# A gated state-space and MLP mix on one core: set-up transposes moved from TensorE to transposing DMAs, and PSUM tiles regrouped

## The chip, the cores and the metric

The kernel runs on one core of a Trainium2 chip. Times are device microseconds (us) of one execution, given as the median of several. Every experiment was run beside the kernel before on the same chip. A ratio is the mean time of one kernel's fast runs over the mean of the other's fast runs of the same rounds, so it is not quite the ratio of the medians quoted. Executions over 1.5% slower than the fastest of the same kernel are left out of the means.

Engine names: PE is TensorE, PEld its weight loads, ACT is ScalarE, DVE is VectorE, POOL is GpSimd, SP is SyncE, which here only issues DMAs. "ACTq" and "SPq" are the queues from which ACT and SP issue DMAs.

## The reference, cut to what matters

```python
def reference(x, ...):                    # x: 2048 rows x 640, bf16
    g = sigmoid((x * gate_w).sum(-1))     # one gate per row
    # a: complex linear recurrence with 640 states
    h[t] = Lam_bar * h[t-1] + B_bar @ x[t]
    a = 2 * real(C @ h) + x * Dskip
    # b: MLP 640 -> 1728 -> 640 with tanh-GELU
    b = gelu(x @ w1 + b1) @ w2 + b2
    return g * a + (1 - g) * b
```

## The kernel before

Set-up ("the head") loads all inputs, brings x, B and C into transposed form, and makes tables of sines and cosines that turn the complex recurrence into two real scans. Then four groups of 512 rows follow ("the main part"). Each group does the MLP's first product in 14 chunks (`ph`), its activation (`xb`, `x2`, `u`, `sg`, `h1T`), the second product (`pb`, `bg`), five state-space blocks (`ps_bu`, `BB`, `M`, `V`, the scans `GG`, `hTg`), and the last product with the combine (`pa`, `o_sb`). The program is written in that order; a scheduler in the programming framework then places the instructions of each engine in a fixed order.

```python
# loads: ACT's queue issues four, SP's queue four
for hf in range(2):
    (nc.sync if hf == 0 else nc.scalar).dma_start(x_sb[:], x_v[:, hf*HT:(hf+1)*HT, :])
for part, src in enumerate((A_B_re, A_B_im)):
    (nc.sync if part == 0 else nc.scalar).dma_start(b_sb[:], ...)
nc.sync.dma_start(w1_sb...); nc.scalar.dma_start(w2_sb...)
for part, src in enumerate((A_C_re, A_C_im)):
    (nc.sync if part == 0 else nc.scalar).dma_start(c_sb[:], ...)
# ... tables: 10 rounds of ACT ang, four DVE steps, ACT Sin ...
# ... x: 80 PE transposes, PSUM copies by DVE (first half) and ACT (second half)
for part in range(2):                      # B: 50 PE transposes, 10 ACT copies
    for dc in range(NDC):
        for pc in range(NPC):
            nc.tensor.transpose(tp[:, pc*P:(pc+1)*P], b_sb[:, pc, dc*P:(dc+1)*P], ident_bf[:])
        nc.scalar.copy(BT[:, dc, part*NS:(part+1)*NS], tp[:, 0:NS])
# ... C: 50 PE transposes, 10 ACT copies into CT; then CpT from CT (ACT scale, DVE add) ...

# main part
pb = psum_b.tile([P, HALF], F32, name="pb")        # two one-bank buffers, one per half
...
nc.scalar.activation(bg[:, cols], pb[:], AF.Copy, scale=omg[:])
...
pa = psum_a.tile([P, HALF], F32, name="pa")        # one one-bank buffer
...                                                # 10 matmuls + 3 for the skip term
nc.vector.scalar_tensor_tensor(out=o_sb[:, cols], in0=pa[:], scalar=gcol[:], in1=bg[:, cols], ...)
```

Of the kernel before, what the change touches and what calls it, by code (L numbers as in the profile page):

```python
# [9 lines left out]
BF16 = mybir.dt.bfloat16  # L10
F32 = mybir.dt.float32
ALU = mybir.AluOpType
# [8 lines left out]
H1_MULT_ENGINE = "vector"  # L21
X2_ENGINE = "act"
COMBINE_MODE = "dve"
# [19 lines left out]
def kernel(  # L43
# [19 lines left out]
    nc = tc.nc  # L63
# [23 lines left out]

    pool_eng = nc.gpsimd
# [10 lines left out]
    ident_bf = const.tile([P, P], BF16, name="ident_bf")  # L99
    b1c = const.tile([P, NFC], F32, name="b1c")  # L100
# [9 lines left out]
    psum_t_cm = tc.tile_pool(name="psum_t", bufs=3, space=bass.MemoryType.PSUM)  # L110
# [26 lines left out]
    x_sbs = []  # L137
    for hf in range(2):
        x_sb = setup.tile([P, HT, D], BF16, name=f"x_sb{hf}")
        (nc.sync if hf == 0 else nc.scalar).dma_start(x_sb[:], x_v[:, hf * HT:(hf + 1) * HT, :])  # L140
        x_sbs.append(x_sb)
    b_sbs = []
    for part, src in enumerate((A_B_re, A_B_im)):
        b_sb = setup.tile([P, NPC, D], BF16, name=f"b_sb{part}")
        (nc.sync if part == 0 else nc.scalar).dma_start(b_sb[:], src.rearrange("(c p) d -> p c d", p=P))
        b_sbs.append(b_sb)
    nc.sync.dma_start(w1_sb[:, :, 0:F], B_w1.rearrange("(c p) f -> p c f", p=P))
    nc.scalar.dma_start(w2_sb[:, 0:NFULL, :], B_w2[0:NFULL * P, :].rearrange("(c p) d -> p c d", p=P))
    c_sbs = []
    for part, src in enumerate((A_C_re, A_C_im)):  # L150
        c_sb = setup.tile([P, NDC, NS], BF16, name=f"c_sb{part}")
        (nc.sync if part == 0 else nc.scalar).dma_start(c_sb[:], src.rearrange("(c p) s -> p c s", p=P))
        c_sbs.append(c_sb)
# [3 lines left out]
    nc.vector.tensor_copy(ident_bf[:], ident[:])  # L157

# [91 lines left out]
    for hf in range(2):  # L250
        x_sb = x_sbs[hf]
        for dc in range(NDC):
            tp = psum_t.tile([P, HT * P], BF16, name="tp")
            for i in range(HT):
                nc.tensor.transpose(tp[:, i * P:(i + 1) * P], x_sb[:, i, dc * P:(dc + 1) * P], ident_bf[:])  # L255
            if hf == 0:
                nc.vector.tensor_copy(xT[:, dc, hf * HT * P:(hf + 1) * HT * P], tp[:])
            else:
                nc.scalar.copy(xT[:, dc, hf * HT * P:(hf + 1) * HT * P], tp[:])

    for part in range(2):
        b_sb = b_sbs[part]
        for dc in range(NDC):
            tp = psum_t.tile([P, HT * P], BF16, name="tp")
            for pc in range(NPC):
                nc.tensor.transpose(tp[:, pc * P:(pc + 1) * P], b_sb[:, pc, dc * P:(dc + 1) * P], ident_bf[:])
            nc.scalar.copy(BT[:, dc, part * NS:(part + 1) * NS], tp[:, 0:NS])

# [7 lines left out]
    CT = setup.tile([P, NPC, 2 * D], BF16, name="CT")  # L276
    for part in range(2):
        c_sb = c_sbs[part]
        for pc in range(NPC):
            tp = psum_t.tile([P, HT * P], BF16, name="tp")  # L280
            for dcb in range(NDC):
                nc.tensor.transpose(tp[:, dcb * P:(dcb + 1) * P], c_sb[:, dcb, pc * P:(pc + 1) * P], ident_bf[:])
            nc.scalar.copy(CT[:, pc, part * D:(part + 1) * D], tp[:, 0:D])
    for pc in range(NPC):
        ctre = CT[:, pc, 0:D]
        ctim = CT[:, pc, D:2 * D]
        t1 = small.tile([P, D], F32, name="cpt_t1")
# [29 lines left out]

    def ssm_block(pc, tci, hTg):
        tcols = slice(tci * TCW, (tci + 1) * TCW)
        ps = []  # L320
        for part in range(2):
            pt = psum_bu.tile([P, TCW], F32, name=f"ps_bu{part}")
            for dc in range(NDC):
# [172 lines left out]
```

## Time and profile before

| | before |
|---|---|
| time, median of 6 runs | 330.69 us |
| ACT's first computing instruction (Exp) | 25.6 us |
| first `xb`, end of the head | 70.5 us |
| main part, from first `xb` to the end of the span | 258.8 us |

The page of the profiled run: busy time by engine, and the span cut into 40 slices of 8.2 us, with the busy share of each slice in tenths.

```profile
PE 247.3 (75%) x1583; PEld 146.2 (44%) x1604; DVE 240.0 (73%) x474; ACT 184.0 (56%) x341; POOL 14.7 (4%) x24
PE   0132554839999989999997989899889999940574
DVE  2508774485999997668979999982999858199322
ACT  0007999979995268687255685633577574320000
PEclk9999955789999999999999999999999999995599
DMA  7999100000000000100000000100000100000011
```

ACT does nothing for three slices and is then nearly full for the rest of the head; PE fills up from the ninth slice on and DVE from the eleventh.

The timeline (start, duration, engine, line, operation, output and input) says why ACT starts late:

```profile
1.99 5.21 ACTq L148 DMA_DIRECT2D w_sb<-in_B_w_dram  x1
7.23 17.04 ACTq L152 DMA_DIRECT2D c_sb<-in_A_C_im_dram  x1
24.30 1.28 ACT L160 ACT_TABLE_LOAD   x1 [24.30 <-issue]
70.51 0.69 ACT L388 ACTIVATE xb<-ph,b1c 128x512 bf16<-128x512 f32 x1 [1.80 <-issue]
```

The issue of the load of C holds ACT's own queue for 17 us, while the DMA engines work off what was issued before it. ACT computes nothing until that issue is through.

The view by windows (stretch, its length, busy us of PE, PEld, DVE, ACT and POOL, granted clock, DMA share, GB/s) for parts of the head and for the end:

```profile
40.00:50.00 10.00, 5.04 (x40) 4.22 (x40) 6.97 (x16) 9.97 (x17) 0.00 (x0) 0.52 0.00 0
50.00:60.00 10.00, 5.63 (x48) 4.95 (x48) 3.48 (x8) 9.96 (x18) 0.00 (x0) 0.50 0.00 1
290.00:310.00 20.00, 5.14 (x24) 2.35 (x23) 17.02 (x22) 1.13 (x2) 0.00 (x0) 0.66 0.00 0
```

From 40 to 60 us ACT is busy 19.9 of 20 us, so ACT sets the length of the head. Part of that work is copying transposes out of PSUM, as the groups by form show (count, total busy, mean ns):

```profile
L267 ACT COPY BT<-tp 128x640 bf16<-128x640 bf16 x10 | 6.3, 710 | 0.0
L283 ACT COPY CT<-tp 128x640 bf16<-128x640 bf16 x10 | 6.1, 722 | 0.0
L259 ACT COPY xT<-tp 128x1024 bf16<-128x1024 bf16 x5 | 4.9, 1005 | 1.2 <-PE tp L255 1.2
```

### The profile page before, as it was taken

Reading aid. Unit: us, or ns where it says so; the run is one execution under the profiler, and the core shown is the slowest. Engines: PE = TensorE matmul, PEld = TensorE weight load, DVE = VectorE, ACT = ScalarE, POOL = GpSimd, SP = SyncE. Lnnn points to the kernel's source line nnn. Section 1 sums busy time; section 2 is a strip of 40 time slices with the busy share of each in tenths; the row PEclk is TensorE's granted clock in tenths of the full one; section 3 lists DMA queues with packets and bytes.
Section 4 is the critical chain, followed back from the end, with each engine's and each line's share of the span. In section 5 each row is a group of like instructions: output and inputs, shape, how many; then the busy total and the mean of one; then the engine's idle time right before and its main releaser. Section 6 shows DMA issues by size and latency. Waiting matters only on the chain.

```text
span 329.3 us, 4218 instructions
## 1 busy us (share of the span) xinstructions
PE 247.3 (75%) x1583; PEld 146.2 (44%) x1604; DVE 240.0 (73%) x474; ACT 184.0 (56%) x341; POOL 14.7 (4%) x24
## 2 busy tenths in 40 slices
PE   0132554839999989999997989899889999940574
PEld 0132443514335735656743355566445556610353
DVE  2508774485999997668979999982999858199322
ACT  0007999979995268687255685633577574320000
POOL 8710000000000000000000000000000000000000
PEclk9999955789999999999999999999999999995599
DMA  7999100000000000100000000100000100000011
GB/s 218 223 396 365 57 0 1 0 0 2 0 0 3 0 2 21 41 21 0 2 0 1 2 20 20 42 0 3 0 0 22 41 22 0 0 2 0 0 40 40
DMA packets 9667, 13.21 MB, mean 40 GB/s; under 512 B 672, under 2 KB 8992, under 8 KB 9648
## 3 DMA queue, kind: packets, MB, share of 16 engines
q1 hardware_dynamic: 5312, 7.78, 6.9%
q10 hardware_dynamic: 4032, 5.08, 5.1%
q0 software_dynamic: 304, 0.09, 0.5%
q8 instruction: 12, 0.20, 0.2%
q14 instruction: 7, 0.06, 0.1%
HBM read 10.33 MB, written 2.62 MB: 39 GB/s over the span
## 4 chain that ended last, share of the span: by engine, by line
DVE 42%; PE 30%; ACT 4%; issue 2%; ACTq 0%
PE pb L420 12%; PE pa L434 8%; DVE GG L357 6%; DVE u L395 6%; DVE GG L359 6%; PE ph L380 5%; PE ps_bu L324 3%; DVE V L341 3%; DVE o_sb L454 3%; DVE h1T L400 3%; DVE M L338 3%; DVE M L339 3%; DVE N L367 3%; DVE hTg L369 3%; DVE N L368 3%
## 5 line engine op out<-in xcount | busy, mean ns | idle before, releaser
L380 PE MATMUL ph<-xT,w_sb 128*128 128x512 bf16 x269 | 68.5, 384 | 8.9 <-ACT x L391 7.0
L434 PE MATMUL pa<-CpT,hTg 128*128 128x320 bf16 x320 | 52.8, 309 | 24.2 <-DVE hTg L369 17.4
L420 PE MATMUL pb<-w_sb,h1T 128*128 128x320 bf16 x448 | 67.4, 299 | 4.9 <-DVE h1T L400 4.6
L420 PEld LDWEIGHTS <-h1T 128*128 128x128 bf16 x448 | 41.7, 98 | 32.2 <-DVE h1T L400 15.4
L434 PEld LDWEIGHTS <-hTg 128*128 128x128 bf16 x320 | 31.2, 100 | 46.4 <-DVE hTg L369 21.4
L324 PE MATMUL ps_bu<-xT,BT 128*128 128x512 bf16 x190 | 48.8, 379 | 1.0 <-ACT BB L332 0.4
L398 ACT ACTIVATE sg<-u 128x512 bf16<-128x512 bf16 (+1 forms) x56 | 35.7, 640 | 22.6 <-DVE u L395 22.2
L395 DVE SCALAR_TENSOR_TENSOR u<-x,xb 128x512 bf16<-128x512 bf16 (+1 forms) x56 | 38.3, 685 | 12.7 <-ACT x L391 12.5
L388 ACT ACTIVATE xb<-ph,b1c 128x512 bf16<-128x512 f32 (+1 forms) x56 | 38.6, 689 | 15.5 <-PE ph L380 7.5
L380 PEld LDWEIGHTS <-w_sb 128*128 128x128 bf16 x280 | 26.4, 99 | 36.9 <-issue 14.3
L391 ACT ACTIVATE x<-ph,b1c 128x512 bf16<-128x512 f32 (+1 forms) x56 | 38.6, 690 | 0.0
L422 ACT ACTIVATE bg<-pb,omg 128x320 f32<-128x320 f32 x32 | 16.4, 526 | 33.3 <-PE pb L420 33.3
L255 PE MATMUL tp<-ident_bf,x_sb 128*128 128x128 bf16 x80 | 9.0, 305 | 28.4 <-DVE ident_bf L157 15.5
L454 DVE SCALAR_TENSOR_TENSOR o_sb<-pa,gcol,bg 128x320 bf16<-128x320 f32 x32 | 17.5, 546 | 15.9 <-PE pa L443 15.5
L400 DVE TENSOR_TENSOR h1T<-xb,sg 128x512 bf16<-128x512 bf16 (+1 forms) x56 | 23.1, 416 | 5.8 <-ACT sg L398 5.6
L324 PEld LDWEIGHTS <-BT 128*128 128x128 bf16 x200 | 18.9, 97 | 17.3
L338 DVE TENSOR_TENSOR M<-BB,ctab 128x1024 bf16<-128x1024 bf16 x20 | 13.7, 686 | 17.6 <-ACT BB L333 17.4
L255 PEld LDWEIGHTS <-x_sb 128*128 128x128 bf16 x80 | 8.3, 143 | 28.6 <-issue 16.1
L357 DVE TENSOR_TENSOR_SCAN GG<-r,iri,V 128x512 bf16<-128x512 f32 x15 | 19.2, 1281 | 0.3
L359 DVE TENSOR_TENSOR_SCAN GG<-r,iri,V 128x512 bf16<-128x512 f32 x15 | 18.9, 1262 | 0.0
L160 ACT ACT_TABLE_LOAD x1 | 1.3, 1283 | 24.3 <-issue 24.3
L332 ACT CAST BB<-ps_bu 128x512 bf16<-128x512 f32 x20 | 11.9, 596 | 4.7 <-PE ps_bu L324 4.0
(121 smaller groups left out, 266.7 us busy)
## 6 DMA issues: line engine op xcount, KB each, us to landing
out_dram<-o_sb SPq DMA_DIRECT2D x16, 160.0 KB, 1.8
w_sb<-in_B_w_dram SPq DMA_DIRECT2D x1, 2160.0 KB, 24.2
w_sb<-in_B_w_dram ACTq DMA_DIRECT2D x1, 2080.0 KB, 31.0
x_sb<-in_A_x_dram ACTq DMA_DIRECT2D x1, 1280.0 KB, 15.2
x_sb<-in_A_x_dram SPq DMA_DIRECT2D x1, 1280.0 KB, 11.7
b_sb<-in_A_B_re_dram SPq DMA_DIRECT2D x1, 800.0 KB, 17.3
b_sb<-in_A_B_im_dram ACTq DMA_DIRECT2D x1, 800.0 KB, 20.6
c_sb<-in_A_C_re_dram SPq DMA_DIRECT2D x1, 800.0 KB, 27.5
```

Source lines behind the costliest of these rows:

```text
L324: nc.tensor.matmul(pt[:], lhsT=BT[:, dc, part * NS + pc * P: part * NS + (pc + 1) * P], rhs=xT[:, dc, tcols], start=(dc == 0), stop=(dc == ...
L357: nc.vector.tensor_tensor_scan(out=GG[:, 0, :], data0=rb, data1=V[:, 0, :], initial=init_r, op0=ALU.mult, op1=ALU.add)
L359: nc.vector.tensor_tensor_scan(out=GG[:, 1, :], data0=rb, data1=V[:, 1, :], initial=init_i, op0=ALU.mult, op1=ALU.add)
L380: nc.tensor.matmul(ph[:], lhsT=w1_sb[:, dc, fc * P:(fc + 1) * P], rhs=xT[:, dc, tcols], start=(dc == 0), stop=(dc == NDC - 1),)
L388: nc.scalar.activation(xb[:fsz], ph[:fsz], AF.Identity, bias=bcol, scale=1.0)
L391: nc.scalar.activation(x2[:fsz], ph[:fsz], AF.Square, bias=bcol, scale=1.0)
L395: nc.vector.scalar_tensor_tensor(out=u[:fsz], in0=x2[:fsz], scalar=GC0, in1=xb[:fsz], op0=ALU.add, op1=ALU.mult)
L398: nc.scalar.activation(sg[:fsz], u[:fsz], AF.Sigmoid, scale=GK)
L400: heng.tensor_tensor(out=h1T[:fsz, fc, :], in0=xb[:fsz], in1=sg[:fsz], op=ALU.mult)
L420: nc.tensor.matmul(pb[:], lhsT=h1T[:, fc, lcol], rhs=w2_sb[:, fc, cols], start=(fc == 0), stop=(fc == NFC - 1))
L434: nc.tensor.matmul(pa[:], lhsT=hTg[:, j, lcol], rhs=CpT[:, j, cols], start=(j == 0), stop=False)
L454: nc.vector.scalar_tensor_tensor(out=o_sb[:, cols], in0=pa[:], scalar=gcol[:], in1=bg[:, cols], op0=ALU.mult, op1=ALU.add)
```

## The change

The intent is to take the transposes of B, C and half of x off PE and their PSUM copies off ACT by letting transposing DMAs do them, to leave ACT only two loads to issue, and to merge small PSUM evacuations in the main part. PSUM is full (8 banks) before and after. Cut to its core:

```diff
-    (nc.sync if hf == 0 else nc.scalar).dma_start(x_sb[:], ...)      # both halves of x, B, C loaded plainly
+    nc.sync.dma_start(x_sb[:], x_v[:, 0:HT, :])                       # first half of x only
+    nc.scalar.dma_start(w1_sb...); nc.scalar.dma_start(w2_sb...)      # all that ACT issues
+    # 10 DMAs of 640x128 for C, 10 of 640x128 for B, 10 of 512x128 for the second half of x:
+    nc.sync.dma_start_transpose(CT[:, pc, part*D:(part+1)*D], src[:, pc*P:(pc+1)*P])
+    nc.sync.dma_start_transpose(BT[:, dc, part*NS:(part+1)*NS], src[:, dc*P:(dc+1)*P])
+    nc.sync.dma_start_transpose(xT[:, dc, tci*TCW:(tci+1)*TCW], x2d[...])
-    # PE transposes and PSUM copies of x's second half, B and C
+    # CpT is scaled in place, in bf16, without f32 temporaries
+    gw_late = ...   # = 0 * ctab(last table) + gate weights: a copy that exists only after the tables
...
-    psum_h1 bufs=2, psum_a 1 x [P, HALF], psum_b bufs=2 x [P, HALF], bgpool bufs=6, bg f32
+    psum_h1 bufs=1, psum_a 1 x [P, 2, 512], psum_b 1 x [P, 2, 512], bgpool bufs=4, bg bf16
-        nc.scalar.copy(BB[:, 0, :], ps[0][:]); nc.scalar.copy(BB[:, 1, :], ps[1][:])
+        nc.scalar.copy(BB[:], pt[:])                                  # both halves at once
-            nc.scalar.activation(x2[:fsz], ph[:fsz], AF.Square, bias=bcol, scale=1.0)
+            nc.scalar.activation(x2[:fsz], xb[:fsz], AF.Square)       # from SBUF, frees ph earlier
-            nc.scalar.activation(bg[:, cols], pb[:], ...)             # per half
+        nc.scalar.activation(bg[:], pb[:, :, 0:HALF], ...)            # per row tile
-    gate matmuls read gw5b
+    gate matmuls read gw_late
```

Switches for other engine choices that were not in use were also removed.

More of the change, by code (lines that the diff above doesn't have):

```diff
@@ L19 @@
 MAGIC = 12582912.0
-H1_MULT_ENGINE = "vector"
-X2_ENGINE = "act"
-COMBINE_MODE = "dve"
 def swap_mid(ap3: bass.AP) -> bass.AP:
@@ L86 @@
     assert HT * P * 2 <= 2048
-    pool_eng = nc.gpsimd
+    assert NTC % 2 == 0
     const = ctx.enter_context(tc.tile_pool(name="const", bufs=1))
@@ L99 @@
     ident_bf = const.tile([P, P], BF16, name="ident_bf")
+    CT = const.tile([P, NPC, 2 * D], BF16, name="CT")
     b1c = const.tile([P, NFC], F32, name="b1c")
@@ L109 @@
     small = small_cm.__enter__()
-    psum_t_cm = tc.tile_pool(name="psum_t", bufs=3, space=bass.MemoryType.PSUM)
+    psum_t_cm = tc.tile_pool(name="psum_t", bufs=2, space=bass.MemoryType.PSUM)
     psum_t = psum_t_cm.__enter__()
@@ L136 @@
     x_v = x2d.rearrange("(tt p) d -> p tt d", p=P)
-    x_sbs = []
-    for hf in range(2):
-        x_sb = setup.tile([P, HT, D], BF16, name=f"x_sb{hf}")
-        (nc.sync if hf == 0 else nc.scalar).dma_start(x_sb[:], x_v[:, hf * HT:(hf + 1) * HT, :])
-        x_sbs.append(x_sb)
-    b_sbs = []
-    for part, src in enumerate((A_B_re, A_B_im)):
-        b_sb = setup.tile([P, NPC, D], BF16, name=f"b_sb{part}")
-        (nc.sync if part == 0 else nc.scalar).dma_start(b_sb[:], src.rearrange("(c p) d -> p c d", p=P))
-        b_sbs.append(b_sb)
-    nc.sync.dma_start(w1_sb[:, :, 0:F], B_w1.rearrange("(c p) f -> p c f", p=P))
-    nc.scalar.dma_start(w2_sb[:, 0:NFULL, :], B_w2[0:NFULL * P, :].rearrange("(c p) d -> p c d", p=P))
-    c_sbs = []
-    for part, src in enumerate((A_C_re, A_C_im)):
-        c_sb = setup.tile([P, NDC, NS], BF16, name=f"c_sb{part}")
-        (nc.sync if part == 0 else nc.scalar).dma_start(c_sb[:], src.rearrange("(c p) s -> p c s", p=P))
-        c_sbs.append(c_sb)
+    x_sb = setup.tile([P, HT, D], BF16, name="x_sb0")
+    nc.sync.dma_start(x_sb[:], x_v[:, 0:HT, :])
+    nc.scalar.dma_start(w1_sb[:, :, 0:F], B_w1.rearrange("(c p) f -> p c f", p=P))
+    nc.scalar.dma_start(w2_sb[:, 0:NFULL, :], B_w2[0:NFULL * P, :].rearrange("(c p) d -> p c d", p=P))
+    for pc in range(NPC):
+        for part, src in enumerate((A_C_re, A_C_im)):
+            nc.sync.dma_start_transpose(CT[:, pc, part * D:(part + 1) * D], src[:, pc * P:(pc + 1) * P])
+    for dc in range(NDC):
+        for part, src in enumerate((A_B_re, A_B_im)):
+            nc.sync.dma_start_transpose(BT[:, dc, part * NS:(part + 1) * NS], src[:, dc * P:(dc + 1) * P])
+    for tci in range(NTC // 2, NTC):
+        for dc in range(NDC):
+            nc.sync.dma_start_transpose(
+                xT[:, dc, tci * TCW:(tci + 1) * TCW], x2d[tci * TCW:(tci + 1) * TCW, dc * P:(dc + 1) * P]
+            )
     ident = setup.tile([P, P], F32, name="ident")
@@ L157 @@
     nc.vector.tensor_copy(ident_bf[:], ident[:])
+    for dc in range(NDC):
+        tp = psum_t.tile([P, HT * P], BF16, name="tp")
+        for i in range(HT):
+            nc.tensor.transpose(tp[:, i * P:(i + 1) * P], x_sb[:, i, dc * P:(dc + 1) * P], ident_bf[:])
+        if dc % 2 == 0:
+            nc.vector.tensor_copy(xT[:, dc, 0:HT * P], tp[:])
+        else:
+            nc.scalar.copy(xT[:, dc, 0:HT * P], tp[:])
     dtv = cst("dtv")
@@ L248 @@
                 nc.scalar.activation(ctab[:, pc, :], ang[:], AF.Sin)
-    for hf in range(2):
-        x_sb = x_sbs[hf]
-        for dc in range(NDC):
-            tp = psum_t.tile([P, HT * P], BF16, name="tp")
-            for i in range(HT):
-                nc.tensor.transpose(tp[:, i * P:(i + 1) * P], x_sb[:, i, dc * P:(dc + 1) * P], ident_bf[:])
-            if hf == 0:
-                nc.vector.tensor_copy(xT[:, dc, hf * HT * P:(hf + 1) * HT * P], tp[:])
-            else:
-                nc.scalar.copy(xT[:, dc, hf * HT * P:(hf + 1) * HT * P], tp[:])
-    for part in range(2):
-        b_sb = b_sbs[part]
-        for dc in range(NDC):
-            tp = psum_t.tile([P, HT * P], BF16, name="tp")
-            for pc in range(NPC):
-                nc.tensor.transpose(tp[:, pc * P:(pc + 1) * P], b_sb[:, pc, dc * P:(dc + 1) * P], ident_bf[:])
-            nc.scalar.copy(BT[:, dc, part * NS:(part + 1) * NS], tp[:, 0:NS])
     nc.gpsimd.memset(Ddiag[:], 0.0)
@@ L274 @@
         )
-    CT = setup.tile([P, NPC, 2 * D], BF16, name="CT")
-    for part in range(2):
-        c_sb = c_sbs[part]
-        for pc in range(NPC):
-            tp = psum_t.tile([P, HT * P], BF16, name="tp")
-            for dcb in range(NDC):
-                nc.tensor.transpose(tp[:, dcb * P:(dcb + 1) * P], c_sb[:, dcb, pc * P:(pc + 1) * P], ident_bf[:])
-            nc.scalar.copy(CT[:, pc, part * D:(part + 1) * D], tp[:, 0:D])
     for pc in range(NPC):
@@ L286 @@
         ctim = CT[:, pc, D:2 * D]
-        t1 = small.tile([P, D], F32, name="cpt_t1")
-        nc.scalar.activation(t1[:], ctre, AF.Copy, scale=kr2[:, pc:pc + 1])
-        nc.vector.scalar_tensor_tensor(out=CpT[:, 2 * pc, :], in0=ctim, scalar=nki2[:, pc:pc + 1], in1=t1[:],
-                                       op0=ALU.mult, op1=ALU.add)
-        t2 = small.tile([P, D], F32, name="cpt_t2")
-        nc.scalar.activation(t2[:], ctim, AF.Copy, scale=nkr2[:, pc:pc + 1])
-        nc.vector.scalar_tensor_tensor(out=CpT[:, 2 * pc + 1, :], in0=ctre, scalar=nki2[:, pc:pc + 1], in1=t2[:],
-                                       op0=ALU.mult, op1=ALU.add)
+        nc.scalar.activation(CpT[:, 2 * pc, :], ctre, AF.Copy, scale=kr2[:, pc:pc + 1])
+        nc.vector.scalar_tensor_tensor(out=CpT[:, 2 * pc, :], in0=ctim, scalar=nki2[:, pc:pc + 1],
+                                       in1=CpT[:, 2 * pc, :], op0=ALU.mult, op1=ALU.add)
+        nc.scalar.activation(CpT[:, 2 * pc + 1, :], ctim, AF.Copy, scale=nkr2[:, pc:pc + 1])
+        nc.vector.scalar_tensor_tensor(out=CpT[:, 2 * pc + 1, :], in0=ctre, scalar=nki2[:, pc:pc + 1],
+                                       in1=CpT[:, 2 * pc + 1, :], op0=ALU.mult, op1=ALU.add)
+    gw_late = const.tile([P, NDC], BF16, name="gw_late")
+    nc.vector.scalar_tensor_tensor(out=gw_late[:], in0=ctab[:, NPC - 1, 0:NDC], scalar=0.0, in1=gw5b[:],
+                                   op0=ALU.mult, op1=ALU.add)
     psum_t_cm.__exit__(None, None, None)
@@ L305 @@
     h1pool = ctx.enter_context(tc.tile_pool(name="h1pool", bufs=2))
-    bgpool = ctx.enter_context(tc.tile_pool(name="bgpool", bufs=6))
+    bgpool = ctx.enter_context(tc.tile_pool(name="bgpool", bufs=4))
     finp = ctx.enter_context(tc.tile_pool(name="finp", bufs=2))
     psum_bu = ctx.enter_context(tc.tile_pool(name="psum_bu", bufs=1, space=bass.MemoryType.PSUM))
-    psum_h1 = ctx.enter_context(tc.tile_pool(name="psum_h1", bufs=2, space=bass.MemoryType.PSUM))
+    psum_h1 = ctx.enter_context(tc.tile_pool(name="psum_h1", bufs=1, space=bass.MemoryType.PSUM))
     psum_a = ctx.enter_context(tc.tile_pool(name="psum_a", bufs=1, space=bass.MemoryType.PSUM))
-    psum_b = ctx.enter_context(tc.tile_pool(name="psum_b", bufs=2, space=bass.MemoryType.PSUM))
+    psum_b = ctx.enter_context(tc.tile_pool(name="psum_b", bufs=1, space=bass.MemoryType.PSUM))
     psum_g = ctx.enter_context(tc.tile_pool(name="psum_g", bufs=1, space=bass.MemoryType.PSUM))
@@ L319, in ssm_block @@
         tcols = slice(tci * TCW, (tci + 1) * TCW)
-        ps = []
+        pt = psum_bu.tile([P, 2, TCW], F32, name="ps_bu")
         for part in range(2):
-            pt = psum_bu.tile([P, TCW], F32, name=f"ps_bu{part}")
             for dc in range(NDC):
                 nc.tensor.matmul(
-                    pt[:],
+                    pt[:, part, :],
                     lhsT=BT[:, dc, part * NS + pc * P: part * NS + (pc + 1) * P],
@@ L329, in ssm_block @@
                 )
-            ps.append(pt)
         BB = work.tile([P, 2, TCW], BF16, name="BB")
-        nc.scalar.copy(BB[:, 0, :], ps[0][:])
-        nc.scalar.copy(BB[:, 1, :], ps[1][:])
+        nc.scalar.copy(BB[:], pt[:])
         cc = ctab[:, pc:pc + 1, :].to_broadcast([P, 2, TCW])
@@ L389, in mlp1_group @@
             x2 = work.tile([P, TCW], BF16, name="x2")
-            if X2_ENGINE == "act":
-                nc.scalar.activation(x2[:fsz], ph[:fsz], AF.Square, bias=bcol, scale=1.0)
-            else:
-                pool_eng.tensor_tensor(out=x2[:fsz], in0=xb[:fsz], in1=xb[:fsz], op=ALU.mult)
+            nc.scalar.activation(x2[:fsz], xb[:fsz], AF.Square)
             u = work.tile([P, TCW], BF16, name="u")
@@ L398, in mlp1_group @@
             nc.scalar.activation(sg[:fsz], u[:fsz], AF.Sigmoid, scale=GK)
-            heng = pool_eng if H1_MULT_ENGINE == "pool" else nc.vector
-            heng.tensor_tensor(out=h1T[:fsz, fc, :], in0=xb[:fsz], in1=sg[:fsz], op=ALU.mult)
+            nc.vector.tensor_tensor(out=h1T[:fsz, fc, :], in0=xb[:fsz], in1=sg[:fsz], op=ALU.mult)
         return h1T
@@ L408, in fin_B @@
         for dc in range(NDC):
-            nc.tensor.matmul(pg[:], lhsT=xT[:, dc, trow], rhs=gw5b[:, dc:dc + 1],
+            nc.tensor.matmul(pg[:], lhsT=xT[:, dc, trow], rhs=gw_late[:, dc:dc + 1],
                              start=(dc == 0), stop=(dc == NDC - 1))
@@ L414, in fin_B @@
         nc.scalar.activation(omg[:], pg[:], AF.Sigmoid, scale=-1.0)
-        bg = bgpool.tile([P, D], F32, name="bg")
+        bg = bgpool.tile([P, 2, HALF], BF16, name="bg")
+        pb = psum_b.tile([P, 2, 512], F32, name="pb")
         for half in range(2):
             cols = slice(half * HALF, (half + 1) * HALF)
-            pb = psum_b.tile([P, HALF], F32, name="pb")
             for fc in range(NFC):
-                nc.tensor.matmul(pb[:], lhsT=h1T[:, fc, lcol], rhs=w2_sb[:, fc, cols],
+                nc.tensor.matmul(pb[:, half, 0:HALF], lhsT=h1T[:, fc, lcol], rhs=w2_sb[:, fc, cols],
                                  start=(fc == 0), stop=(fc == NFC - 1))
-            nc.scalar.activation(bg[:, cols], pb[:], AF.Copy, scale=omg[:])
+        nc.scalar.activation(bg[:], pb[:, :, 0:HALF], AF.Copy, scale=omg[:])
         return gcol, bg
@@ L429, in fin_A @@
         o_sb = finp.tile([P, D], BF16, name="o_sb")
+        pa = psum_a.tile([P, 2, 512], F32, name="pa")
         for half in range(2):
             cols = slice(half * HALF, (half + 1) * HALF)
-            pa = psum_a.tile([P, HALF], F32, name="pa")
+            pah = pa[:, half, 0:HALF]
             for j in range(2 * NPC):
-                nc.tensor.matmul(pa[:], lhsT=hTg[:, j, lcol], rhs=CpT[:, j, cols],
+                nc.tensor.matmul(pah, lhsT=hTg[:, j, lcol], rhs=CpT[:, j, cols],
                                  start=(j == 0), stop=False)
@@ L443, in fin_A @@
                 nc.tensor.matmul(
-                    pa[:, lo - half * HALF: hi - half * HALF],
+                    pa[:, half, lo - half * HALF: hi - half * HALF],
                     lhsT=xT[:, dc, trow],
@@ L448, in fin_A @@
                 )
-            if COMBINE_MODE == "pool":
-                ag = finp.tile([P, HALF], F32, name="ag")
-                nc.scalar.activation(ag[:], pa[:], AF.Copy, scale=gcol[:])
-                pool_eng.tensor_tensor(out=o_sb[:, cols], in0=ag[:], in1=bg[:, cols], op=ALU.add)
-            else:
-                nc.vector.scalar_tensor_tensor(out=o_sb[:, cols], in0=pa[:], scalar=gcol[:], in1=bg[:, cols],
-                                               op0=ALU.mult, op1=ALU.add)
+            nc.vector.scalar_tensor_tensor(out=o_sb[:, cols], in0=pah, scalar=gcol[:], in1=bg[:, half, :],
+                                           op0=ALU.mult, op1=ALU.add)
         nc.sync.dma_start(out2d[trow, :], o_sb[:])
```

## The prediction

> **What bounds the kernel now.** Two parts. (1) A head of 70 us: the first group's first evacuation (ACT xb) runs at 70.5 us in the timeline. ScalarE sets its length. Its queue issues four loads and is held by them until 24.3 us (the page shows ACT's first instruction idle 24.3 "issue"; the last issue alone, c_sb, takes 17 us). Then it is nearly full: 8.75, 9.97, 9.96 and 8.70 us busy in the four 10-us stretches from 30 to 70 (view by windows). (2) A main part of about 259 us, bound alternately by VectorE (19.97 of 20 us in 90 to 110 and 190 to 210) and TensorE (19.8 of 20 in 130 to 150, with unbroken 11.4 us pb blocks on the chain of waits). The chain is 42% DVE, 30% PE.
>
> **What the change does to the head.** It takes from ACT the BT copies (10 x 710 ns = about 6.3 us by groups), CT copies (6.1) and three of five 1.0 us xT copies (2.9): 15 us. It leaves ACT two loads to issue, about 2300 descriptors' worth of rows, fewer than were queued when issue began to stall, so ACT should start when log_dt lands, about 10 us: 14 us earlier. VectorE's angle work (10 rounds of about 1.95 us) then paces the tables: about 20 us. In exchange the SP queue transposes 4.6 MB in 30 DMAs. No transposing DMA is in this trace. The Trainium skill, "DMA: Bandwidth & Descriptors", section "Latency and other measured facts", gives 261 GB/s for a transpose with a non-contiguous middle dimension; that would be about 18 us. I doubt it with 256-byte rows: from 1280-byte packets at about 220 GB/s and 3456-byte ones at about 396 (page, GB/s line) I estimate a fixed 45 ns a packet, so about 75 GB/s, 60 us in total. Between the two, CT lands at 22 to 42 us, BT at 30 to 65 us. CpT scaling (ACT and DVE about 9 us each) waits for CT and may hold up ACT's in-order queue. If transposes were free the head would lose 29 us; I expect 24 to 26.
>
> **Main part.** Saved on ACT: BB in one copy (estimate 0.2 us x20), bg in one (0.25 us x16), squares from bf16 (about 0.05 us x56): 10 us in all, off the chain. Lost: ph has one buffer, so each chunk runs matmuls 1.08 us, then xb 0.69 and two handovers, about 2.2 us against about 2.0 now (ACT sum); pb is one pair of banks, so about 1.2 us of PE wait after each of 16 row tiles unless ps_bu or ph matmuls fill it; the pb blocks will break up. Pa is a pair, which lets TensorE do the second half under the first combine: about 1 us in the tail. VectorE work per group is unchanged. Net estimate: +1 us (between -6 and +12).
>
> **Predicted:** 307 us; 8 in 10 between 290 and 327. Faster by over 2%: 0.82; within 2%: 0.12; slower: 0.06.
>
> **What would show it.** ACT's first compute near 10 us instead of 25.6; first xb between 38 and 52 us; GB/s above 100 through 15 to 45 us; 50 PE transposes for b and 50 for c gone, 40 for x left; main part from first xb to end within 253 to 271 us; pb blocks of 28 matmuls.
>
> **What would make it wrong.** Transposing DMAs at 40 GB/s or less: BT would land past 80 us, the state-space blocks, which begin at 78 us now, would start no earlier, and the gain would vanish. ACT or DVE queued behind a wait for CT. A second sigmoid/sine table exchange. Single-buffered ph and pb starving TensorE more than 12 us. On the other side, a better interleave of state-space work into the broken pb blocks could give 10 us more.

## More of the kernel before

Timeline, kernel before, near the end:

```profile
317.45 1.52 PE L434 MATMUL pa<-CpT,hTg 128*128 128x320 bf16 x10 [0.64 <-DVE o_sb L454]
319.14 0.55 DVE L454 SCALAR_TENSOR_TENSOR o_sb<-pa,gcol,bg 128x320 bf16<-128x320 f32 x1 [1.75 <-PE pa L443]
319.75 1.52 PE L434 MATMUL pa<-CpT,hTg 128*128 128x320 bf16 x10 [0.64 <-DVE o_sb L454]
```

Each half of a row tile takes 2.30 us (317.45 to 319.75), of which PE waits 0.64 us for the combine to empty `pa`.

## The result, and the profile after

| | before | after |
|---|---|---|
| time, median | 330.68 us (16 runs) | 304.24 us (8 runs) |
| ACT's first computing instruction | 25.6 us | 9.1 us |
| first `xb` | 70.5 us | 47.4 us |
| main part, from first `xb` to the end | 258.8 us | 254.6 us |

The ratio of the fast runs is 0.9214, 95% interval 0.9197 to 0.9231. The profiled spans are 329.3 and 302.0 us; of the 27.3 us between them, 23.1 lie ahead of the first `xb` and 4.2 after it.

The page after (slices of 7.6 us):

```profile
PE 234.4 (78%) x1442; PEld 131.3 (43%) x1464; DVE 236.2 (78%) x473; ACT 164.1 (54%) x282; POOL 14.7 (5%) x24
PE   0070128898889899898899997888999998798564
DVE  3599995999999743999982549999963599999421
ACT  1088978786874145697642456773434588431100
PEclk9996555999999999999999999999999999999999
DMA  7999765400000001000000110000001100000001
```

ACT works from the second slice on. The DMA row now stays busy for eight slices in place of five. At the end the clock no longer drops. The timeline of the head:

```profile
1.95 1.28 ACT L164 ACT_TABLE_LOAD   x1 [1.95 <-issue]
9.12 0.21 ACT L164 ACTIVATE dtv<-ldt 128x5 f32<-128x5 f32 x1 [5.88 <-DVE ldt L114]
42.15 1.27 SPq L143 DMA_TRANSPOSE BT<-in_A_B_im_dram  x1
43.47 14.28 SPq L146 DMA_TRANSPOSE xT<-in_A_x_dram  x10
47.40 0.69 ACT L364 ACTIVATE xb<-ph,b1c 128x512 bf16<-128x512 f32 x1
48.10 1.28 ACT L384 ACT_TABLE_LOAD   x1
```

ACT's first table load now comes at 1.95 us where it came at 24.30. ACT waits only for the constants, computes at 9.12 us, and reaches the first `xb` at 47.40 us. The issue of one transposing DMA occupies SP's queue for 1.27 us, and the last BT is issued at 42.15 us.

The head can be added up on ACT. The windows from its first computing instruction to the first `xb`, in the kernel before and then in the kernel after:

```profile
25.60:70.50 44.90, 21.77 (x172) 17.28 (x173) 30.58 (x94) 41.27 (x67) 0.00 (x0) 0.77 0.21 70
9.10:47.40 38.30, 10.65 (x54) 5.86 (x56) 35.11 (x108) 27.43 (x45) 6.98 (x10) 0.71 0.84 191
```

ACT starts 16.5 us earlier and has 13.8 us less to do (41.27 against 27.43), but in between it stands idle for 10.87 us where it was 3.63, so 7.2 are lost again: 16.5 + 13.8 - 7.2 = 23.1 us, the whole gain of the head.

The tail, in the same three steps as before:

```profile
289.63 1.52 PE L407 MATMUL pa<-CpT,hTg 128*128 128x320 bf16 x10 [0.64 <-DVE o_sb L422]
291.38 0.55 DVE L422 SCALAR_TENSOR_TENSOR o_sb<-pa,gcol,bg 128x320 bf16<-128x320 f32 x1 [1.81 <-PE pa L416]
291.98 1.52 PE L407 MATMUL pa<-CpT,hTg 128*128 128x320 bf16 x10 [0.70 <-DVE o_sb L422]
```

The half still takes 2.35 us, although its two halves now lie in two banks. And on the chain of waits (start, duration, what), two row tiles of `pb` inside the main part:

```profile
154.41 3.96 PE pb L392 x28
159.26 3.96 PE pb L392 x28
```

A block of 28 matmuls ends at 158.37, the next begins at 159.26: 0.89 us of waiting, where the chain of the kernel before has one unbroken block of 84:

```profile
153.17 11.41 PE pb L420 x84
```

Such waits were few: of PE's idle time, the profile puts 1.7 us in all, in three places, down to the evacuation of `pb`, and 1.9 us to that of `ph`.

The two stretches at the end can also be compared by windows. Before, 290 to 310 us: 5.14 us of PE work and a granted clock of 0.66. After:

```profile
270.00:290.00 20.00, 14.15 (x105) 9.69 (x105) 13.34 (x18) 2.08 (x3) 0.00 (x0) 1.00 0.03 9
```

In the kernel before PE waited 6.03 and then 5.29 us for VectorE's `hTg` ahead of the last `pa` matmuls and did ten of them in 2.82 us in place of 1.52, at a granted clock of 0.50:

```profile
308.50 2.82 PE L434 MATMUL pa<-CpT,hTg 128*128 128x320 bf16 x10 [0.64 <-DVE o_sb L454]
```

The next ten took 2.13 us, so the low clock cost 1.9 us in these twenty. In the kernel after, the last two waits of this kind are 0.93 and 1.75 us, and the clock stays at 0.99 to 1.00. The Trainium skill, "TensorE: Matmul & The Clock Gate", Part 1: The HAM clock gate, ties half clock to idleness, and the trace agrees. From the first to the last `o_sb` of the final group it is 18.2 us before (307.9 to 326.1) and 16.2 us after (282.1 to 298.3), so about 2 of the main part's 4.2 us lie there. The other 2 are not separated: VectorE's main-part instructions stand in the same place in only 73 of 304 cases before and after, so that the merged copies and the new order act together.

### The profile page after: what moved, and what is told of

Read it like the earlier page. It is cut to its first block, busy times and chain, and to the rows that moved or that the text cites. A ratio compares the mean times of both kernels' runs of the same rounds, so it can differ in the third digit from the quotient of the medians.

```text
span 302.0 us, 3878 instructions
## 1 busy us (share of the span) xinstructions
PE 234.4 (78%) x1442; PEld 131.3 (43%) x1464; DVE 236.2 (78%) x473; ACT 164.1 (54%) x282; POOL 14.7 (5%) x24
## 4 chain that ended last, share of the span: by engine, by line
DVE 58%; PE 27%; DMA 5%; ACT 5%; issue 2%; DVEq 0%; ACTq 0%
PE pa L407 12%; DVE u L368 8%; PE pb L392 7%; DVE GG L333 7%; DVE GG L335 7%; DMA x_sb<-in_A_x_dram 5%; DVE h1T L372 5%; DVE V L317 4%; DVE M L315 4%; DVE M L314 4%; PE ph L356 4%; DVE hTg L345 3%; DVE N L343 3%; DVE N L344 3%; DVE o_sb L422 2%
## 5 line engine op out<-in xcount | busy, mean ns | idle before, releaser
L392 PE MATMUL pb<-w_sb,h1T 128*128 128x320 bf16 x448 | 71.4, 299 | 13.5 <-DVE h1T L372 11.3
L302 PE MATMUL ps_bu<-xT,BT 128*128 128x512 bf16 x193 | 56.6, 394 | 22.2 <-DMA BT<-in_A_B_re_dram 19.2
L356 PE MATMUL ph<-xT,w_sb 128*128 128x512 bf16 x265 | 71.3, 384 | 2.9 <-ACT xb L364 1.9
L392 PEld LDWEIGHTS <-h1T 128*128 128x128 bf16 x448 | 43.4, 98 | 45.1 <-DVE h1T L372 23.9
L407 PE MATMUL pa<-CpT,hTg 128*128 128x320 bf16 x320 | 51.8, 299 | 7.7 <-DVE o_sb L422 4.8
L368 DVE SCALAR_TENSOR_TENSOR u<-x,xb 128x512 bf16<-128x512 bf16 (+1 forms) x56 | 38.2, 681 | 13.8 <-ACT x L366 11.2
L422 DVE SCALAR_TENSOR_TENSOR o_sb<-pa,gcol,bg 128x320 bf16<-128x320 f32 x32 | 17.6, 550 | 27.0 <-PE pa L416 26.4
L366 ACT ACTIVATE x<-xb 128x512 bf16<-128x512 bf16 (+1 forms) x56 | 35.1, 627 | 0.8
L394 ACT ACTIVATE bg<-pb,omg 128x640 bf16<-128x640 f32 x16 | 12.7, 791 | 40.0 <-PE pb L392 40.0
L372 DVE TENSOR_TENSOR h1T<-xb,sg 128x512 bf16<-128x512 bf16 (+1 forms) x56 | 23.1, 413 | 1.5 <-ACT sg L371 1.2
L309 ACT CAST BB<-ps_bu 128x1024 bf16<-128x1024 f32 x20 | 20.0, 1002 | 0.0
L157 PE MATMUL tp<-ident_bf,x_sb 128*128 128x128 bf16 x40 | 4.6, 305 | 17.3 <-DMA x_sb<-in_A_x_dram 17.3
L317 DVE TENSOR_TENSOR V<-M,M 128x1024 bf16<-128x1024 bf16 x20 | 13.7, 685 | 0.2
L343 DVE TENSOR_TENSOR N<-GG,ctab 128x1024 bf16<-128x1024 bf16 x20 | 13.6, 682 | 0.1
## 6 DMA issues: line engine op xcount, KB each, us to landing
x_sb<-in_A_x_dram SPq DMA_DIRECT2D x1, 1280.0 KB, 16.5
```

Of the source, the lines that this page charges most:

```text
L302: nc.tensor.matmul(pt[:, part, :], lhsT=BT[:, dc, part * NS + pc * P: part * NS + (pc + 1) * P], rhs=xT[:, dc, tcols], start=(dc == 0), st ...
L356: nc.tensor.matmul(ph[:], lhsT=w1_sb[:, dc, fc * P:(fc + 1) * P], rhs=xT[:, dc, tcols], start=(dc == 0), stop=(dc == NDC - 1),)
L366: nc.scalar.activation(x2[:fsz], xb[:fsz], AF.Square)
L368: nc.vector.scalar_tensor_tensor(out=u[:fsz], in0=x2[:fsz], scalar=GC0, in1=xb[:fsz], op0=ALU.add, op1=ALU.mult)
L372: nc.vector.tensor_tensor(out=h1T[:fsz, fc, :], in0=xb[:fsz], in1=sg[:fsz], op=ALU.mult)
L392: nc.tensor.matmul(pb[:, half, 0:HALF], lhsT=h1T[:, fc, lcol], rhs=w2_sb[:, fc, cols], start=(fc == 0), stop=(fc == NFC - 1))
```

## The experiments

### e1 and e2: either part alone

e1 is the new head with the old main part, e2 the old head with the new main part; the code was cut where the set-up pools are closed. In e1 the old main part takes the gate's weights from the late copy, as the new head prepares them.

```diff
 e1:  after.py up to the closing of the set-up pools, then before.py's pools, groups and combine (gw5b -> gw_late)
 e2:  before.py up to the closing of the set-up pools, then after.py's main part (gw_late -> gw5b)
```

> The head (everything up to the first group) of the kernel after, the main part of the kernel before. Theory H: the gain is the shorter head, 23 of the 27 us (first xb at 47.4 us instead of 70.5), and the rest of the program simply starts earlier. H expects first xb at 46 to 49 us and a time of 306 to 311 us. Rival M: the gain comes from the changed main part (merged copies, squares from bf16, changed PSUM buffers) and the head's work was hidden or is made up for later; M expects 320 us or more.

> The head of the kernel before, the main part of the kernel after. H expects first xb at 69 to 72 us and 323 to 329 us. M expects 312 us or less. If e1 and e2 gain together clearly more or less than 27 us, the two parts interact.

| | time | ratio to before (95%) | first `xb` | main part |
|---|---|---|---|---|
| before | 330.51 | | 70.5 | 258.8 |
| e1 | 317.93 | 0.9614 (0.9597 to 0.9631) | 47.8 | 268.3 |
| e2 | 327.24 | 0.9895 (0.9862 to 0.9928) | 70.5 | 255.8 |
| after | 304.24 | 0.9214 (0.9197 to 0.9231) | 47.4 | 254.6 |

e2 came out as the head theory (H) said: the new main part is worth about 3 us, 1%, with its own order (four runs, 326.3 to 328.1 us). e1 did not come out as either theory said. Its head is as short as expected, but its main part is 9.5 us longer than in the kernel before, with the same main code. The two parts sum to 15.9 us, not to 26.4.

The order of VectorE's instructions explains where to look. Compared over 304 main-part instructions in the traces, e2's order is exactly that of the kernel after, while e1 has only 147 of 304 in the place that they have in the kernel before. In e1, the scans of the last group run from 255 to 290 us, after the last `h1T` of the group at 252 us; in the kernel before they run from 252 to 304 us, overlapping with MLP chunks until the last `h1T` at 273 us. In e1 that leaves PE with little to do near the end. So e2 against after is the clean measurement of the head (same order, 327.24 to 304.24: 23.0 us, and first `xb` 23.1 us earlier), and e1 is not one of the main part. e4 tests this reading.

### e3: only the issue of loads moved away from ACT

```diff
-            (nc.sync if hf == 0 else nc.scalar).dma_start(x_sb[:], ...)   # same for b_sb and c_sb
+            nc.sync.dma_start(x_sb[:], ...)
-    nc.sync.dma_start(w1_sb[:, :, 0:F], ...)
+    nc.scalar.dma_start(w1_sb[:, :, 0:F], ...)
```

> The kernel before, but with only w1 and w2 loaded from the ACT queue; x, B and C all from the SP queue; every PE transpose and every PSUM copy stays. Theory H1: about half of the head's gain is ACT being released from the stalled issue of loads (first compute at 9 us instead of 25.6). H1 expects ACT's first compute near 9 us, first xb at 56 to 62 us and 316 to 322 us. Rival H2: only the copies and transposes taken off the engines count, because ACT then waits for x, B and C to land anyway; H2 expects first xb at 67 us or later and 327 to 331 us.

Measured: 321.95 us, ratio 0.9739 (0.9716 to 0.9763). The first `xb` moved from 70.5 to 62.0 us, and VectorE's main-part order is that of the kernel before in all 304 places. The line of the `xb` instructions in e3 gives durations (min, median, max) and first and last start:

```profile
L388 ACT ACTIVATE xb<-ph,b1c x56: 667/687/807, 62.0 to 261.5; 128x512 bf16<-128x512 f32 x52, 64x512 bf16<-64x512 f32 x4
```

So 8.5 us of the head come from four changed issue queues alone, with every transpose and copy kept. H1's range was met at its upper edge; H2 fell. The prediction had put 14 us on this term.

Where the rest went shows in the window from ACT's first computing instruction to the first `xb` in e3:

```profile
9.20:62.00 52.80, 25.08 (x205) 20.25 (x206) 35.95 (x104) 41.53 (x67) 7.03 (x10) 0.83 0.51 159
```

ACT does the same work as before (41.5 against 41.3 us) and starts 16.4 us earlier, but idles 11.3 us in place of 3.6. The longest wait, 6.2 us, is that of its second computing instruction for `ar` and `th` from VectorE: it runs at 15.6 us in e3 and at 26.0 us in the kernel before, 10.4 us earlier and not 16.4. The kernel after has nearly the same wait (6.1 us).

### e8: what sets the rate of the transposing DMAs

```diff
-    for tci in range(NTC // 2, NTC):
-        for dc in range(NDC):
-            nc.sync.dma_start_transpose(xT[:, dc, tci*TCW:(tci+1)*TCW], x2d[...])   # 10 of 512 rows
+    for dc in range(NDC):
+        nc.sync.dma_start_transpose(xT[:, dc, HT*P:L], x2d[HT*P:L, dc*P:(dc+1)*P])   # 5 of 1024 rows
```

> The kernel after, with the second half of x transposed by 5 DMAs of 1024 rows instead of 10 of 512. Measures what sets the rate of the transposing DMAs. Theory I: each instruction costs a fixed 1.3 us on the issuing queue; the 5 issues take 1.3 us each and the last lands about 6.5 us earlier. Rival R: the rows (256-byte packets) set it; the 5 issues take about 2.6 us each once the queue is full and the last lands at about the same time. Both expect 303 to 306 us, as the second half of x is first needed after 100 us.

Measured: 303.92 us (a single run of state unknown). The issue line of the timeline in e8:

```profile
43.78 6.72 SPq L145 DMA_TRANSPOSE xT<-in_A_x_dram  x5
```

Five issues take 6.72 us, 1.34 us each, for 262,144 bytes each: 195 GB/s. In the kernel after, ten take 14.28 us, 1.43 us each (the median issue 1.26 us, one of them 2.10), for 131,072 bytes each: 92 GB/s. The transfers follow the issues: by windows of 2 us the DMA traffic ends before 54 us in e8 and before 60 in the kernel after. Between 512 and 1024 rows, twice the rows cost hardly more time, so a cost per instruction sets the rate there (theory I), and the 256-byte row does not (rival R). Longer instructions need not go on gaining: from 46 to 48 us the DMA engines are busy 0.95 of the time in e8 (197 GB/s), against 0.47 (106 GB/s) in the kernel after. An estimate from e8's figures, 16 engines at 0.95 and 197 GB/s in 256-byte packets, is 20 ns a packet. The total does not move, because nothing waits for this half of x.

### e4 and e5: the late copy of the gate's weights taken out

`gw_late` looks like a trifle: a 128x5 multiply by zero and add. e4 is e1 with the gate's matmuls reading the loaded weights again; e5 is the kernel after with the same edit.

```diff
-            nc.tensor.matmul(pg[:], lhsT=xT[:, dc, trow], rhs=gw_late[:, dc:dc + 1],
+            nc.tensor.matmul(pg[:], lhsT=xT[:, dc, trow], rhs=gw5b[:, dc:dc + 1],
```

> As e1 (new head, old main part), but the gate's matmuls read the loaded weights again and not the late copy. Offline, VectorE's order of work in the main part is then nearly that of the kernel before (188 of 210 compared instructions in the same place; e1 has 92). Theory O: e1 lost 9.5 us in its main part only because its instruction order changed. O expects first xb at 46 to 50 us, a main part of 257 to 262 us and 306 to 311 us in all. Rival B: the old main part's buffers are slower behind the new head (state-space work starts while B is landing); B expects 315 to 320 us as in e1.

> The kernel after, with the late copy of the gate's weights taken out again. Theory G: the late copy is there to keep the gate's sigmoid from loading its table between the sines; without it more table loads of 1.28 us appear in the head and it grows by 3 to 10 us. Rival N: it only shifts the order; table loads stay at 3 and the time is within 3 us of 304.

e5 measured 313.33 us, ratio 0.9483 (0.9463 to 0.9504): 9.1 us slower than the kernel after. First `xb` is at 55.9 us in place of 47.4. The table loads on ACT, timeline of e5, four of eleven:

```profile
23.59 1.28 ACT L384 ACT_TABLE_LOAD   x1
25.08 1.28 ACT L252 ACT_TABLE_LOAD   x1
41.70 1.28 ACT L386 ACT_TABLE_LOAD   x1
44.40 1.28 ACT L252 ACT_TABLE_LOAD   x1
```

L384 and L386 are the gate's sigmoids, L252 a table's sine: each sigmoid placed between sines costs two loads. The kernel after has 3 loads, of which 2 precede the first `xb`; e5 has 11, all ahead of it. Nine more at 1.28 us make 11.5 us; ACT's busy time in the head grows by 11.8 us, its idle time shrinks by 3.3, and the head grows by 8.5. Theory G holds.

e4 measured 315.39 us, which lies in the range that the rival (B) gave. The total alone would have confirmed the wrong theory. Its first `xb` is at 55.6 us, for the same 11 table loads, so O's expectation for the head failed; but its main part is 313.3 - 55.6 = 257.7 us, as O said (257 to 262), against 268.3 in e1 and 258.8 in the kernel before. With nearly the old order, the old main part is as fast behind the new head as behind the old one. That e1 lost its 9.5 us to the order is therefore well supported, though the edit that restored the order also moved the gate's work and delayed the head by 8 us, past the landing of B. Rival B's cause, state-space work held up while B lands, is contradicted by e1's own trace: its first scan comes 15.2 us after the first `xb` (15.4 in the kernel before), and the first group's scans end no later either; the loss comes after that.

### e6, e7: `pa` and `pb` as two one-bank tiles

```diff
 e6:
-        pa = psum_a.tile([P, 2, 512], F32, name="pa")
         for half in range(2):
-            pah = pa[:, half, 0:HALF]
+            pa = psum_a.tile([P, HALF], F32, name=f"pa{half}")
 e7:
-        pb = psum_b.tile([P, 2, 512], F32, name="pb")
         for half in range(2):
+            pb = psum_b.tile([P, HALF], F32, name=f"pb{half}")
             ...
+            nc.scalar.activation(bg[:, half, :], pb[:], AF.Copy, scale=omg[:])
-        nc.scalar.activation(bg[:], pb[:, :, 0:HALF], AF.Copy, scale=omg[:])
```

> The kernel after, with pa as two one-bank tiles in place of one two-bank tile. In the tail of the kernel after each half of a row tile takes 2.30 us, the same as before the change: the matmuls of the second half wait for the combine of the first. Theory T: the wait is on the tile, not on the bank; with two tiles a half takes about 1.7 us and the tail from the first to the last o_sb shrinks from 16.2 to about 12.5 us; 298 to 302 us unless the order costs it. Rival: the wait is set by something else (the output tile or gate); the half stays at 2.3 us.

> The kernel after, with pb as two one-bank tiles, each evacuated by its own ACT instruction. On the chain of the kernel after, blocks of 28 pb matmuls (3.96 us) follow each other with gaps of 0.9 us for the evacuation. Theory P: single-buffered pb costs about 0.9 us for each row tile that nothing fills, some 3 a group: 296 to 302 us. Rival F: the gaps are filled elsewhere by work that must be done anyway; 303 to 306 us.

e6 measured 302.26 us, ratio 0.9158 (0.9130 to 0.9187), a little below the kernel after. Its last row tiles take 1.50 us a half, and PE no longer waits for the combine:

```profile
292.20 1.52 PE L407 MATMUL pa<-CpT,hTg 128*128 128x320 bf16 x10
293.70 1.52 PE L407 MATMUL pa<-CpT,hTg 128*128 128x320 bf16 x10
```

So the wait was on the tile as the framework tracks it, not on the bank. But the order changed: part of the last group's `pb` blocks moved behind the scans into the tail, and the final group's `o_sb` steps spread over 20.9 us in place of 16.2. The tail expectation failed although the mechanism held.

e7 measured 305.12 to 308.55 us in its three fast runs (the profiled one, 310.04 us, counts as slow), ratio 0.9294 (0.9246 to 0.9342). In the profiled run its `pb` blocks are partly unbroken again, but its order differs (122 of 304 places agree with the kernel after), and three sets of ten `pa` matmuls near its end take 2.82 us each in place of 1.52. That trace is of the slow run, so how much of this the fast runs share is not shown. By its fast runs e7 is about 1% slower than the kernel after: neither P's nor F's range was met in all of them. Alone, neither edit tells what its own wait costs, because each also gives the scheduler another order.

### e9, e10: what binds the new head

e9 moves the zeroing of `Ddiag` from POOL to DVE. In the kernel after, a tiny cast on DVE lasts 2.73 us while POOL does this memset, and the chain that leads to the tables (`ar`) comes after it:

```profile
10.19 2.77 POOL L254 MEMSET Ddiag<- 128x3200 bf16 x1
10.26 2.73 DVE L114 CAST Lre<-Lre_bf 128x5 f32<-128x5 bf16 x1 [1.10 <-DMA Lre_bf<-in_A_Lambda_re_dram]
15.26 0.15 DVE L166 TENSOR_TENSOR ar<-dtv,Lre 128x5 f32<-128x5 f32 x1
```

The Trainium skill, "SBUF — State Buffer", section "Who interferes with whom", says that DVE's two-port modes and GpSimd exclude each other over a shared port pair, and counts casts among the operations that can use them; a cast held for the length of a POOL memset agrees with it.

```diff
-    nc.gpsimd.memset(Ddiag[:], 0.0)          # after the tables
+    nc.vector.memset(Ddiag[:], 0.0)          # ahead of the small loads
```

> The kernel after, with the zeroing of Ddiag moved from the Pool engine (2.8 us from 10.2 us on, during which a VectorE cast of 128x5 takes 2.73 us instead of 0.17) to VectorE before anything has landed. Offline the main part's VectorE order is that of the kernel after. Theory V: the head is now bound by VectorE from the first landed constants on, so ar and th come 2.5 us earlier and the first xb with them: 44 to 46 us and 301 to 303 us. Rival X: the head hangs on the first half of x (landed at 17.3 us), as the chain of waits of the kernel after begins; then first xb and time stay within 0.7 us.

Measured: 307.65 us, ratio 0.9321 (0.9290 to 0.9353), slower than the kernel after. The cast is short now (0.17 us), but the scheduler placed the building of the index ramp, which had run while DVE waited for constants, behind the casts, and a copy of `xT` that waited 1.15 us for PE ahead of `ar`. `ar` came at 19.35 us, 4.1 us later, and the first `xb` at 51.3 us, 3.9 us later. The edit did not do what it was meant to do, so neither expectation applies. What it does show, in one case, is a delay of `ar` by 4.1 us that passes through to the first `xb` (3.9 us) and to the end (about 3.5 us) almost in full; VectorE's main-part order is that of the kernel after.

e10 leaves out the second step of the `CpT` scaling, ten VectorE instructions of 0.88 us:

```diff
-        nc.vector.scalar_tensor_tensor(out=CpT[:, 2 * pc, :], in0=ctim, scalar=nki2[:, pc:pc + 1], in1=CpT[:, 2 * pc, :], ...)
-        nc.vector.scalar_tensor_tensor(out=CpT[:, 2 * pc + 1, :], in0=ctre, scalar=nki2[:, pc:pc + 1], in1=CpT[:, 2 * pc + 1, :], ...)
```

> Wrong result on purpose: the kernel after without the second step of the CpT scaling (10 VectorE instructions of 0.88 us in the head); ScalarE's step stays, the order of the rest is that of the kernel after. Theory V (the head is bound by VectorE, 10 us of 10 busy in 30 to 40): first xb 6 to 9 us earlier, 38.5 to 41.5 us, but the first state-space block still waits for BT, whose last transpose lands at 46 us, so that the whole gains only 2 to 7 us. Rival: ScalarE or the DMA order sets the head; first xb stays at 45 us or later and the time within 2 us of 304.

The computation is wrong; the comparison passed all the same, because the missing term is small beside its tolerance. Measured: 303.74 us, ratio 0.9180 (0.9158 to 0.9201), first `xb` at 46.3 us: 1.1 us earlier where theory V asked for 6 to 9. A window of the kernel after:

```profile
25.00:35.00 10.00, 0.61 (x1) 0.11 (x1) 10.00 (x22) 10.00 (x16) 0.00 (x0) 0.51 0.76 143
```

The same window of e10:

```profile
25.00:35.00 10.00, 0.46 (x1) 0.11 (x1) 7.53 (x22) 10.00 (x16) 0.00 (x0) 0.58 0.80 144
```

DVE was full and is no longer, but ACT is still full from 25 to 35 us. Theory V, that DVE alone binds the head, fell, and both ranges of the rival (ACT or the order of the DMAs) were met. ACT is the likelier of the two: in e10's head it waits for VectorE and, 0.5 us, for PE, never for a DMA. But no run relieved ACT alone, so that both engines limit the new head at once is argued, not shown.

### e11, e12: the edits together

e11 is e6, e7 and e9 in one kernel; e12 leaves e9's edit out again.

```diff
 e11: pa -> pa0, pa1;  pb -> pb0, pb1;  Ddiag zeroed on DVE
 e12: pa -> pa0, pa1;  pb -> pb0, pb1
```

> The kernel after with three edits together: pa and pb as two one-bank tiles each, Ddiag zeroed on VectorE. If the unbroken pb blocks (11.4 us for 84) and the 1.5 us halves of pa add up, 295 to 300 us. If the static order decides, as in e7, it is 300 to 308 us and no edit's saving can be read off the total.

> The kernel after with pa and pb as two one-bank tiles each, Ddiag left on the Pool engine. Offline its VectorE order in the main part is e11's and its head is that of the kernel after. If head and main part add up, with first xb at 47.3 us as in the kernel after and a main part of 245.8 us as in e11, the span is about 293 us and the time 293.5 to 296.5 us. If the early VectorE zeroing in e11 was not what cost its head 4.4 us, the time stays at 298 to 300 us.

e11 measured 298.79 us, ratio 0.9043 (0.9026 to 0.9060), in spite of a first `xb` at 51.8 us: its main part is 245.8 us. e12 has e11's VectorE order in the main part and measured 294.99 us (5 fast runs), ratio 0.8931 (0.8917 to 0.8945), with the first `xb` at 47.1 us. Head and main part added up as expected (47.3 + 245.8 = 293.1; the span is 292.8). It is faster than both kernels.

The chain of waits of e12 has the `pb` block whole again:

```profile
89.41 11.41 PE pb L392 x84
```

and the timeline of its tail has the combines under the next matmuls:

```profile
281.34 1.52 PE L407 MATMUL pa<-CpT,hTg 128*128 128x320 bf16 x10
281.60 0.55 DVE L422 SCALAR_TENSOR_TENSOR o_sb<-pa,gcol,bg 128x320 bf16<-128x320 f32 x1 [1.11 <-PE pa L416]
282.84 1.52 PE L407 MATMUL pa<-CpT,hTg 128*128 128x320 bf16 x10
```

A half takes 1.50 us (281.34 to 282.84) and PE no longer waits for the combine. Of the 9 us that the two edits gain together, 6.4 lie in the tail: the final group's `o_sb` steps spread over 9.9 us in place of 16.2. That is near what the `pa` edit alone promises there, seven halves at 0.85 us, 6.0 us; in e6 it was hidden by `pb` blocks that the order had moved into the tail. PE's waits for the evacuation of `pb` fall only from 1.7 to 0.5 us. The rest is not separated from the order, which is another one again.

## Why the prediction was right, point by point

- **Total.** 307 us was predicted and 304.24 measured, inside the range of 290 to 327. Faster by over 2% was the likeliest class, at 0.82, and it came. That the number lies within 3 us is in part luck: the head was expected to shorten by 24 to 26 us and the main part to grow by 1, and both were off in opposite directions (23.1 us, and 4.2 less).
- **Head shorter by 24 to 26 us, first `xb` between 38 and 52 us.** Measured 23.1 us and 47.4 us; e2 against after confirms that the head alone is worth 23.0 us. Right in size, but by terms that offset each other, as the next points show.
- **ACT released from issuing, 14 us.** The start did come 16 us earlier (9.1 against 25.6 us), but e3 shows that this alone shortens the head by 8.5 us. Mis-sized: the prediction counted the earlier start in full and left out that ACT then waits, 6.2 us for `ar` and `th` alone, and idles 11.3 us in place of 3.6. The rest of the head's 23.1 us, 14.6, goes with the 13.8 us of work taken from ACT (predicted: 15 us of copies, less 3 to 5 us for the transposing DMAs); this split is one of several possible, since e3 measured the release without the rest.
- **VectorE's angle work then paces the tables.** At most half right. ACT and DVE are both full (10.00 of 10 us from 25 to 35), and e10 shows that taking `CpT` off DVE wins only 1.1 us.
- **Transposing DMAs: between an estimate of 18 us, at the rate that the Trainium skill gives in "DMA: Bandwidth & Descriptors", section "Latency and other measured facts", and 60 us from a packet estimate.** The last of C was issued at 29.0 us and landed, at the median of 3.8 us, at about 33 us (predicted 22 to 42) and the last of B at about 46 us (30 to 65). The reason given for doubt, 256-byte packets at 45 ns each, is wrong: e8 shows about 1.3 us per instruction at 512 and at 1024 rows, and some 20 ns a packet. Bandwidth above 100 GB/s lasted through 45 us, as said.
- **A second sigmoid/sine table exchange** stood among the things that could go wrong. What the prediction missed is that one line of the change, `gw_late`, prevents it, and that this line is worth 9.1 us (e5). It was not priced at all.
- **Main part 253 to 271 us, net +1.** Measured 254.6 us, 4.2 less than before. The `pb` blocks did break into 28, with 0.89 us between those shown, but the 1.2 us of wait after each of 16 row tiles came only three times, 1.7 us in all. For `ph` the profile shows 1.9 us of PE waiting for `xb`; what its single buffer costs by itself was not tried.
- **"Pa is a pair, which lets TensorE do the second half under the first combine: about 1 us in the tail."** This step failed. A half stays at 2.30 to 2.35 us, because the wait is on the tile and not on the bank; e6 and e12 show 1.50 us with two tiles. The tail's gain of about 2 us came with the granted clock, which no longer drops there (1.9 us of slow matmuls before).

## What to carry to other kernels

Before moving work off an engine, look at what that engine's queue does first: four load issues on ACT's queue held its start until 24 us, and changing the queue alone gained 8.5 us of 330. A two-bank PSUM tile is one object to the framework's waits; where a producer should run ahead of a consumer bank by bank, give each bank its own tile and compare the trace, because the total also contains whatever new order the scheduler chose. When two variants differ, check first whether their instruction order differs: here a changed order went with a loss of 9.5 us (e1), and a total (e4) agreed with the wrong theory.

## What the Trainium skill lacked or had wrong

- "DMA: Bandwidth & Descriptors", section "Latency and other measured facts", gives a transposing DMA with a non-contiguous middle dimension 261 GB/s. Here it was 92 GB/s with 131,072 bytes an instruction and 195 GB/s with 262,144. The section gives a rate only; here the time went by instruction, 1.3 to 1.4 us each.
- "VectorE: DVE Perf Modes", section "The three transpose paths", gives the DMA path 1309 ns for one 128x128 block. Here about that much was the issue of a whole instruction, of four blocks (1.26 us for 512x128), of five (1.27 us for 640x128) as of eight (1.30 us for 1024x128).
- "Advanced Engine Details and Errata", section "X-Bar Transpose (TRN2)", says that transposing DMAs are as fast as regular ones. Plain loads (rows of 1280 and 3456 bytes) reached 396 GB/s in a slice of the page before, and transposing ones (256-byte rows) by themselves about 195. A plain load of 256-byte rows was not run.
- "ScalarE: Activation LUTs", section "What ACT_TABLE_LOAD costs", puts a switch of tables at 2.66 us, 1283 ns for the load and about 1380 ns for a drain. Every load here took 1.28 us, and no drain shows beside it: in the kernel before ACT's previous instruction ends at 27.65 us, the load runs from 27.67, and the next instruction starts at 28.96. "ScalarE activation tables: per-element evaluation and per-set limits", section "What a function is on this engine", has two functions of different sets one load (1283 ns) apart, which fits.
- No page that was read says that a two-bank PSUM tile is waited for as a whole by the framework. Here that costs 0.85 us for each half of a row tile in the tail (2.35 us against 1.50 with two tiles in e6).
